# A fused attention and two-expert kernel: first expert in three passes, fewer early weights, more attention buffers

## The chip, the cores and the metric

One core of one Trainium2 chip runs the whole program. The metric is the device time of one execution in microseconds (us). The kernel before has a median of 669.59 us over three runs (669.0 to 670.03).

## What is computed

Shapes: batch 2, 8 heads, 768 positions, head size 64, so 1536 tokens of width 512. All weights come as float64 and are turned into float32 on the chip.

```python
keep = is_global | is_local            # 8 global keys, the last 96 positions
scores = np.where(keep, q @ k.T / 8 + bias, -1e9)
x = softmax(scores) @ v                # (1536, 512)
h = x @ w_in                           # w_in (512, 2048)
x = (h * np.tanh(softplus(h))) @ w_out # first expert, w_out (2048, 512)
g, val = x @ w_gate, x @ w_val         # (512, 1536) each
out = (g * sigmoid(g) * val) @ w_out2  # second expert, w_out2 (1536, 512)
```

## The kernel before, in words

**Order of the work.** The program is first written down as a list of operations (`op`), each with the engines that can do it and a cost in ns. `Plan.order` then places them on the engines in the order of a due time: the sum of the TensorE costs written down before the operation (`nominal`), plus 7000 for other engines, made earlier where a later operation needs it in time. An operation that can run on several engines (a "copy" on ACT or DVE, say) is placed on the one that the plan holds free sooner. Each engine and SP's DMA queue then run their own list in that fixed order and wait for each other by semaphores. Buffers come from pools (`Pool`), handed out in the order in which they were asked for; an operation that finds none is held back, and so are those behind it in that pool.

**Attention.** 12 tiles of 128 positions, 6 per batch, each in two halves of 4 heads (24 half tiles, `s`). For each half: `transp` (L440) turns k and q of the tile by 4 TensorE transposes into one bank and copies the bank to `kq`, which has places 0 and 1 for the keys of the last two tiles and place 2 for the queries (L454, on ACT or DVE); `qk` (L469) makes the scores against the keys of this tile and the one before (L480); `softmax` (L485) adds the bias and takes the row limit on DVE (L499) and the exponential on ACT (recorded at helper line L329); `turn` (L528) transposes the weights by 4 to 8 TensorE transposes (L541) into two banks and copies them to `et`; `spread` (L508) turns the reciprocals of the row sums (L522) into `rs`; `pv` (L551) multiplies with v (L562), scales (L570) and splits the result into a high and a low part of the token block `xt`. A copy by ACT is recorded at L352, one by DVE or POOL at L349. The transposes and pv take their PSUM banks from one pool, `t_p`, with 3 banks. Banks 0 to 3 hold scores, bank 7 is for warm-up matmuls.

**Warm-up.** `warm_up` (L590) writes down 6 matmuls on zeros (L596) that run first, and LATE = 24 more with a due time after everything else: the plan places one wherever it holds TensorE idle.

**Weights.** A unit is 128 x 512 float64 numbers: one column block of w_in, or the matching rows of w_out. `convert` (L392) brings it in by a DMA of 512 KB (L402), takes the absolute value on ACT (L404), does four steps on DVE (L887 to L890) and splits it into a high and a low part (L349 or L352, then L362) in a slot of `w_p`. There are NWA = 13 slots from the start, and NWB = 15 more that take the memory of attention when all of attention is over (`switch`). In the attention loop `units_to` writes down up to 9 units, one per tile from s = 5 on.

**Experts.** Tokens go in 3 chunks of 512. A job is one chunk and one block of 128 hidden columns. `hidden` makes 12 matmuls from `x` (three products of the high and low parts, 4 blocks of the width), then the activation on ACT and DVE (`mish`, L698, or `swiglu`), then 12 matmuls into four output banks `ys` (`out_b`, L759). All of these matmuls are recorded at helper line L373. Jobs of the first expert go in pairs (`jobs_b`, L736), which share the activation's table loads. The 16 column blocks of the first expert go in two passes of 8: for each pass all three chunks, and for each chunk the 8 blocks. The first job of a pass and chunk starts the output banks, the last one empties them: in the first pass by a copy to `st` and a DMA to `part1`, in the second by a DMA from `part1`, an addition on DVE and the split into `xt` on POOL. The 12 blocks of the second expert go in two passes of 6.

What sets how early a job can run: its `h_p` banks (banks 0 to 3, once all scores are done), the output banks (4 to 7, after `switch`), and its units. Unit 2f is the block f of w_in, unit 2f + 1 that of w_out. Requests for `h_p` banks are served in the order of the jobs.

```python
453  copy(lambda: kq.t[:, prs, c:3:2 - c, :], ...)        # keys to place c, queries to place 2
483  pe(emit, [(kq, (c, hf)) for c in (2, 0, 1)[:nb + 1]], ...)
599  op([("P", 216, emit)], ..., prio=-1e5 if i < first else 1e6)
827  units_to(min(9, max(0, (s - 3)//2)))
845  for fs, whole in ((range(0, FA), False), (range(FA, F1), True)):
846      for c in range(NCH):
847          seq += [(1, c, f, f == fs[0], f == fs[-1], whole) for f in fs]
```

Of the kernel before, what the change touches and what calls it, by code (L numbers as in the profile page):

```python
# [219 lines left out]
def kernel(  # L220
# [21 lines left out]
    KD = DM // P  # L242
    CH = 512
    NCH = NTOK // CH
    FA = F1 // 2
    NWA = 13
    NWB = 15
    NST = 2
    WARM = 6
    LATE = 24  # L250
    EDGE = 104
    SPARE = 2500.0
    SCALE = -1.0 / float(D) ** 0.5
# [18 lines left out]
    def fixed(pool, shape, dtype, name):  # L272
        return Buf(t=pool.tile(shape, dtype, name=name))

    def slots(pool, n, shape, dtype, name):
        return [Slot(pool.tile(shape, dtype, name=f"{name}{i}")) for i in range(n)]
# [15 lines left out]
    h_p = Pool([])  # L292
    y_p = Pool([])

    kq = fixed(asb, [P, NP, 3, P], F32, "kq")
    e_p = Pool(slots(asb, 3, [P, 4, 256], F32, "e"))
    et_p = Pool(slots(asb, 5, [P, 2, 2, P], F32, "et"))
    rb_p = Pool(slots(asb, 2, [P, NP, P], F32, "rb"))
    raw_in = {n: Pool(slots(asb, 2, [P, H, D], F32, "in_" + n)) for n in "qkvu"}
    xs_p = Pool(slots(asb, 2, [P, NP, P], F32, "xs"))  # L300
    rs_p = Pool(slots(asb, 1, [P, NP * P], F32, "rs"))
    bias = fixed(asb, [P, H, 3 * P], BF16, "bias")
    bias0 = fixed(asb, [P, H, P], BF16, "bias0")
    kg = fixed(asb, [P, NP, WG], F32, "kg")
# [4 lines left out]
    sm_p = Pool(slots(asb, 3, [P, H], F32, "sm"))  # L309
    asb.tile([P, EDGE], I32, name="edge")  # L310

    asb_pools = [*raw_in.values(), e_p, sm_p, et_p, rb_p, xs_p, rs_p, t_p, warm_p]
    asb_fixed = [bias, bias0, kq, kg, mn, nt, nf, chk]

    def of_attention(o):
# [17 lines left out]
    def dve(emit, r, w, n=512, fast_=False):  # L333
        return op([("V", (150 if fast_ else 68) + (0.52 if fast_ else 1.045) * n, emit)], r, w)

    def dma(emit, r, w, kb=256, prio=None):
        return op([("S", 150 + kb * 4.2, emit)], r, w, lat=2000.0, prio=prio)

    def pe(emit, r, w, mms, n=512, shape="FF", spare=0.0):
        o = op([("P", mms * (max(n, 230) / 2.4 + 13.5), emit)], r, w)  # L340
        o.shape, o.spare = shape, spare
        return o
# [4 lines left out]
    def copy(o, i, r, w, scale=1.0, n=512, psum_in=False, on="AVG"):  # L347
        def dve_pool(eng):
            return lambda: eng.tensor_scalar(out=o(), in0=i(), scalar1=scale, scalar2=0.0, op0=ALU.mult, op1=ALU.add)  # L349

        alts = [("A", (50 if psum_in else 92) + 0.835 * n,
                 lambda: nc.scalar.activation(out=o(), in_=i(), func=AF.Copy, scale=scale)),  # L352
                ("V", (68 + 1.045 * n) if psum_in else (180 + 0.52 * n), dve_pool(nc.vector))]
        if not psum_in:
            alts.append(("G", 160 + 0.88 * n, dve_pool(nc.gpsimd)))
        o_ = op(some(alts, on), r, w)
        o_.port = not psum_in
        return o_
# [56 lines left out]
    def load(i, names="qk"):  # L415
        b, t = tiles[i]
        for nm, src in (("q", q), ("k", k), ("v", v)):
            if nm not in names:
                continue
            x = plan.buf(raw_in[nm])  # L420
            raws[nm, i] = x
            for hs in (slice(0, 4), slice(4, 8)) if i == 0 else (slice(0, H),):
                dma(lambda x=x, src=src, hs=hs: nc.sync.dma_start(
                    out=x.t[:, hs], in_=src[b, hs, t * P:(t + 1) * P, :].rearrange("h s d -> s h d")), [],
                    [(x, hf) for hf in range(hs.start // 4, hs.stop // 4)], kb=32 * (hs.stop - hs.start),
                    prio=-1e6 + hs.start + 9 * (nm == "v") if i == 0 else None)
# [13 lines left out]
    def transp(i, hf):  # L440
        b, t = tiles[i]
        xk, xq = raws["k", i], raws["q", i]
        ps = plan.buf(t_p)
        c = t % 2
        prs = slice(2 * hf, 2 * hf + 2)

        def emit():
            for p in range(4):
                x = xq if p % 2 else xk
                h = 4 * hf + p // 2 * 2  # L450
                nc.tensor.transpose(ps.t[:, p * P:(p + 1) * P], x.t[:, h:h + 2, :].rearrange("s h d -> s (h d)"), ident)  # L451

        pe(emit, [(xk, hf), (xq, hf)], [(ps, 0)], 4, 128)
        copy(lambda: kq.t[:, prs, c:3:2 - c, :], lambda: ps.t.rearrange("p (a b s) -> p a b s", a=2, b=2), [(ps, 0)],  # L454
             [(kq, (c, hf)), (kq, (2, hf))], psum_in=True, on="AV")

    def move_k(i, hf):
        b, t = tiles[i]
# [10 lines left out]
    def qk(s):  # L469
        i, hf = divmod(s, 2)  # L470
        b, t = tiles[i]
        nb = 1 if t == 0 else 2
        banks = scs[s] = [plan.buf(sc_p[0]), plan.buf(sc_p[1])]

        def emit():
            for p in range(2):
                pr = 2 * hf + p
                for j in range(2):
                    ro = slice(64 * j, 64 * j + 64)
                    nc.tensor.matmul(out=banks[j].t[:, p * 256:p * 256 + nb * P], lhsT=kq.t[ro, pr, 2, :],  # L480
                                     rhs=kq.t[ro, pr, 0:nb, :].rearrange("p b s -> p (b s)"), start=True, stop=True)

        pe(emit, [(kq, (c, hf)) for c in (2, 0, 1)[:nb + 1]], [(banks[0], 0), (banks[1], 0)], 8, 230, "RR")

    def softmax(s):  # L485
        i, hf = divmod(s, 2)
# [272 lines left out]
    def out_b(kind, c, f, first, last, whole, g, w, ds):  # L759
        for d in ds:  # L760
            if first:
                ys[d] = plan.buf(y_p)
            y = ys[d]
            blk = slice(d * P, (d + 1) * P)

            def emit(y=y, blk=blk):
                if kind == 1:
                    mm3(y.t, lambda a: w.t[:, a, blk], lambda b: g.t[:, b, :], first, last)
                else:
                    mm3(y.t, lambda a: g.t[:, a, blk], lambda b: w.t[:, b, :], first, last)  # L770

            pe(emit, [(w, 0), (w, 1), (g, 0), (g, 1)], [(y, 0)], 3, CH, spare=SPARE)
            if not last:
                continue
            st = plan.buf(st_p)
            Y, T = [(y, 0)], [(st, 0)]
            if not whole:
                part, pk = (part1, p1) if kind == 1 else (part2, p2)
                copy(lambda st=st: st.t, lambda y=y: y.t, Y, T, scale=1.0 if kind == 1 else 0.5, psum_in=True, on="AV")
                dma(lambda st=st, d=d, part=part: nc.sync.dma_start(out=part[c, d], in_=st.t), T, [(pk, (c, d))])  # L780
            elif kind == 1:
                dma(lambda st=st, d=d: nc.sync.dma_start(out=st.t, in_=part1[c, d]), [(p1, (c, d))], T)
                dve(lambda st=st, y=y: tt(st.t, y.t, st.t, ALU.add), Y, T)
                ks = lambda a: [(xt[c], (a, d, t)) for t in range(CH // P)]
                copy(lambda d=d: xt[c].t[:, 0, d, :], lambda st=st: st.t, T, ks(0), on="G")
                arith(lambda d=d: xt[c].t[:, 1, d, :], lambda st=st: st.t,
                      lambda d=d: xt[c].t[:, 0, d, :].bitcast(F32), ALU.subtract, T + ks(0), ks(1), on="G")
            else:
                dma(lambda st=st, d=d: nc.sync.dma_start(out=st.t, in_=part2[c, d]), [(p2, (c, d))], T)
                dve(lambda st=st, y=y: nc.vector.scalar_tensor_tensor(out=st.t, in0=y.t, scalar=0.5, in1=st.t,  # L790
                                                                      op0=ALU.mult, op1=ALU.add), Y, T)
                r = c * CH + d * P
                dma(lambda st=st, r=r: nc.sync.dma_start(out=out[r:r + P, :], in_=st.t), T, [])


    setup()
    load(1)
    transp(0, 0)
    transp(0, 1)
# [2 lines left out]
    def units_to(n):  # L802
        while n_units[0] < min(n, len(units), freed[0] + room[0]):
            convert(n_units[0])
            n_units[0] += 1

    NS = 2 * NTL
    for s in range(NS + 2):
        i, hf = divmod(s, 2)
        if s < NS:  # L810
            if hf == 0:
                load_previous(i)
                if i + 1 < NTL:
                    load(i + 1, "v")
            qk(s)
            softmax(s)
            move_k(i, hf)
            if i + 1 < NTL:
                transp(i + 1, hf)
            if hf == 1 and i + 2 < NTL:  # L820
                load(i + 2)
        if 0 <= s - 1 < NS:
            turn(s - 1)
            if s % 2 == 0:
                spread(s // 2 - 1)
                pv(s // 2 - 1)
        units_to(min(9, max(0, (s - 3)//2)))
        if s == NS:
            flag()
    def switch():  # L830
# [11 lines left out]
       grow=[(w_p, wb_slots), (st_p, st_slots), (y_p, bank[4:8])])  # L842
    room[0] += NWB
    seq = []
    for fs, whole in ((range(0, FA), False), (range(FA, F1), True)):
        for c in range(NCH):
            seq += [(1, c, f, f == fs[0], f == fs[-1], whole) for f in fs]
    for fs, whole in ((range(0, F2 // 2), False), (range(F2 // 2, F2), True)):
# [281 lines left out]
```

## Time and profile before

| | us |
|---|---|
| median of 3 runs | 669.59 (669.0 to 670.03) |
| the profiled execution, its own time | 668.81 |
| its span, first to last instruction | 667.0 |
| first expert matmul starts | 99.53 |
| last expert matmul ends | 660.57 |

A row of the profile names the engine (PE is TensorE's matmuls, PEld its weight loads, DVE VectorE, ACT ScalarE, POOL GpSimd, SP the DMA queue), the line, and `out<-in` by the program's names. Matmuls are pipelined: the mean duration of one is longer than the distance from start to start, so the time that a run of matmuls takes is read from the chain of waits or from the starts.

### The profile page before, as it was taken

What the parts mean: (1) busy time and instruction counts of PE and PEld (TensorE: products, weight loads), DVE (VectorE), ACT (ScalarE), POOL (GpSimd) and SP (SyncE); (2) the same over time, 40 slices, a digit from 0 to 9 for tenths busy, and PEclk for the clock granted to TensorE, in tenths of its full rate; (3) what the DMA queues carried; (4) which work ended last, traced back from release to release, by engine and by line L of the source; (5) the groups of instructions that cost most, each with busy time, mean ns of one, the idle gap of its engine ahead of it and who ended that gap; (6) DMA issues with size and microseconds to landing.
All of it is one profiled execution on the core that took longest, in us unless ns stands there. A gap on an engine that the chain in (4) does not pass through costs nothing.

```text
span 667.0 us, 9142 instructions
## 1 busy us (share of the span) xinstructions
PE 652.8 (98%) x3343; PEld 535.9 (80%) x3343; DVE 410.5 (62%) x831; ACT 351.1 (53%) x636; POOL 109.7 (16%) x168
## 2 busy tenths in 40 slices
PE   8998999999999999999999999999999999999996
PEld 6876778878888888888888888888888888888884
DVE  5788887888678685797688877222842223323313
ACT  6999997878766776867685333212521211111111
POOL 4343542112111110150251410000000000000000
PEclk9999999999999999999999999999999999999999
DMA  8677641433325234243132224100400300300301
GB/s 197 171 174 179 168 129 63 127 127 130 117 70 179 73 132 153 94 143 124 51 127 93 97 70 142 72 1 1 148 10 16 111 0 17 111 0 17 110 1 68
DMA packets 80068, 63.58 MB, mean 95 GB/s; under 512 B 48272, under 2 KB 68752, under 8 KB 80016
## 3 DMA queue, kind: packets, MB, share of 16 engines
q1 hardware_dynamic: 80016, 62.93, 30.8%
q8 instruction: 28, 0.46, 0.3%
q14 instruction: 24, 0.20, 0.1%
HBM read 53.48 MB, written 9.44 MB: 94 GB/s over the span
## 4 chain that ended last, share of the span: by engine, by line
PE 89%; ACT 5%; DVE 2%; DMA 2%; issue 1%; SPq 0%; ACTq 0%; DVEq 0%
PE bank L373 78%; PE bank L562 3%; PE bank L480 3%; PE bank L541 2%; PE bank L451 2%; DMA raw<-in_moe_w_out_dram 1%; ACT e L329 1%; ACT et L352 1%; PE bank L596 1%; PE bank L522 1%; ACT kq L352 1%; ACT cv L404 1%; DMA in_k<-in_k_dram 1%; ACT u L329 0%; DVE a L362 0%
## 5 line engine op out<-in xcount | busy, mean ns | idle before, releaser
L373 PE MATMUL bank<-x,wa 128*128 128x512 f32 x756 | 180.8, 390 | 1.3 <-DVE a L362 1.3
L373 PEld LDWEIGHTS bank<-x,wa 128*128 128x128 f32 x756 | 141.7, 188 | 31.3 <-DVE a L362 1.7
L373 PE MATMUL bank<-x,wb 128*128 128x512 f32 x684 | 163.5, 390 | 0.0
L373 PEld LDWEIGHTS bank<-x,wb 128*128 128x128 f32 x684 | 128.4, 188 | 26.6
L329 ACT ACTIVATE u<-bank 128x512 f32<-128x512 f32 x84 | 49.9, 594 | 133.4 <-PE bank L373 133.2
L352 ACT ACTIVATE g<-a 128x512 fp32r<-128x512 f32 x64 | 40.3, 632 | 109.9 <-DVE a L729 93.7
L727 DVE SCALAR_TENSOR_TENSOR a<-u,bank 128x512 f32<-128x512 f32 x36 | 24.7, 687 | 92.0 <-ACT u L329 91.9
L362 DVE TENSOR_TENSOR g<-a,g 128x512 fp32r<-128x512 f32 x84 | 61.0, 738 | 22.5 <-ACT g L352 19.3
L373 PE MATMUL bank<-wa,g 128*128 128x512 f32 x288 | 70.2, 389 | 0.0
L373 PE MATMUL bank<-g,wb 128*128 128x512 f32 x288 | 69.0, 389 | 0.0
L373 PE MATMUL bank<-g,wa 128*128 128x512 f32 x288 | 68.9, 390 | 0.0
L373 PEld LDWEIGHTS bank<-g,wa 128*128 128x128 f32 x288 | 54.1, 188 | 11.2
L373 PEld LDWEIGHTS bank<-g,wb 128*128 128x128 f32 x288 | 54.1, 188 | 11.2
L373 PEld LDWEIGHTS bank<-wa,g 128*128 128x128 f32 x288 | 54.1, 188 | 11.2
L729 DVE TENSOR_TENSOR a<-a,bank 128x512 f32<-128x512 f32 x36 | 24.7, 687 | 49.4 <-PE bank L373 49.3
L889 DVE SCALAR_TENSOR_TENSOR cv<-raw,cv 128x512 int32<-128x512 int32 x68 | 48.4, 717 | 0.9
L404 ACT ACTIVATE cv<-raw 128x512 f32<-128x512 f32 x68 | 44.8, 665 | 7.7 <-DMA raw<-in_moe_w_out_dram 4.6
L887 DVE TENSOR_SCALAR cv<-cv 128x512 f32<-128x512 f32 x68 | 35.0, 516 | 22.3 <-ACT cv L404 22.1
L890 DVE SCALAR_TENSOR_TENSOR cv<-raw,cv 128x512 int32<-128x512 int32 x68 | 47.5, 706 | 0.8
L329 ACT ACTIVATE e<-e,mn 128x256 f32<-128x256 f32 (+1 forms) x96 | 46.1, 490 | 1.1 <-DVE mn L499 0.8
L349 POOL TENSOR_SCALAR g<-a 128x512 fp32r<-128x512 f32 x20 | 13.2, 659 | 202.6 <-DVE a L729 125.8
L362 DVE TENSOR_TENSOR a<-bank,u 128x512 f32<-128x512 f32 x48 | 31.1, 686 | 18.9 <-ACT u L329 18.4
(92 smaller groups left out, 748.0 us busy)
## 6 DMA issues: line engine op xcount, KB each, us to landing
raw<-in_moe_w_out_dram SPq DMA_DIRECT2D x28, 512.0 KB, 3.3
raw<-in_moe_w_in_dram SPq DMA_DIRECT2D x16, 512.0 KB, 3.8
raw<-in_moe_w_gate_dram SPq DMA_DIRECT2D x12, 512.0 KB, 3.7
raw<-in_moe_w_val_dram SPq DMA_DIRECT2D x12, 512.0 KB, 3.6
part<-st SPq DMA_DIRECT2D x12, 256.0 KB, 2.1
part<-sb SPq DMA_DIRECT2D x12, 256.0 KB, 2.1
st<-part SPq DMA_DIRECT2D x12, 256.0 KB, 2.8
sb<-part SPq DMA_DIRECT2D x12, 256.0 KB, 3.7
```

The source lines that it names most:

```text
L329: nc.scalar.activation(out=o(), in_=i(), func=func, scale=scale, **args)
L352: lambda: nc.scalar.activation(out=o(), in_=i(), func=AF.Copy, scale=scale)),
L362: return lambda: eng.tensor_tensor(out=o(), in0=x(), in1=y(), op=alu)
L373: nc.tensor.matmul(out=o, lhsT=lhs(a), rhs=rhs(b), start=first and i == 0, stop=last and i == len(PASSES) - 1)
L404: op([("A", 520, lambda: nc.scalar.activation(out=wf(), in_=hi().bitcast(F32), func=AF.Abs))], R, W_)
L480: nc.tensor.matmul(out=banks[j].t[:, p * 256:p * 256 + nb * P], lhsT=kq.t[ro, pr, 2, :], rhs=kq.t[ro, pr, 0:nb, :].rearrange("p b s -> p ( ...
L562: nc.tensor.matmul(out=o.t[64 * j:64 * j + 64, p * P:(p + 1) * P], lhsT=v_of(c).t[:, 2 * p + j, :], rhs=et4[p].t[:, c, j, :], start=c == 0 ...
L727: dve(lambda: nc.vector.scalar_tensor_tensor(out=a.t, in0=u.t[:, 0], scalar=1.0, in1=hg.t, op0=ALU.add, op1=ALU.mult), U + [(hg, 0)], A_)
L729: dve(lambda: nc.vector.tensor_tensor(out=a.t, in0=a.t, in1=hv.t, op=ALU.mult), [(hv, 0)], A_)
L887: lambda: ts(out=f(), in0=f(), scalar1=F64_LOW, scalar2=F64_HIGH, op0=ALU.max, op1=ALU.min),
L889: lambda: stt(out=w(), in0=high(), scalar=-0x40000000, in1=w(), op0=ALU.bitwise_and, op1=ALU.bitwise_or),
L890: lambda: stt(out=w(), in0=low(), scalar=29, in1=w(), op0=ALU.logical_shift_right, op1=ALU.bitwise_or),
```

## The change

The first expert's 16 column blocks go in passes of 4, 4 and 8 instead of 8 and 8. The middle pass brings the partial sum in, adds and writes it back (12 more DMA loads, additions and DMA stores of 256 KB). Up to 5 units instead of 9 are written down in the attention loop, from s = 7 on instead of s = 5, and the slots that exist from the start are 10 instead of 13 (18 instead of 15 come after attention). The 12 KB per partition that this frees pay for a fourth buffer of `e`, a sixth of `et`, a second of `rs` and a second place for turned queries. There are 6 late warm-up matmuls instead of 24, with a due time near 0 through the operation that follows them, and when they are done bank 7 joins `t_p` as its fourth bank.

```diff
--- before.py
+++ after.py
@@ -242,12 +242,12 @@
     KD = DM // P
     CH = 512
     NCH = NTOK // CH
-    FA = F1 // 2
-    NWA = 13
-    NWB = 15
+    PASSES1 = (0, 4, 8)
+    NWA = 10
+    NWB = 18
     NST = 2
     WARM = 6
-    LATE = 24
+    LATE = 6
     EDGE = 104
     SPARE = 2500.0
     SCALE = -1.0 / float(D) ** 0.5
@@ -292,13 +292,13 @@
     h_p = Pool([])
     y_p = Pool([])
 
-    kq = fixed(asb, [P, NP, 3, P], F32, "kq")
-    e_p = Pool(slots(asb, 3, [P, 4, 256], F32, "e"))
-    et_p = Pool(slots(asb, 5, [P, 2, 2, P], F32, "et"))
+    kq = fixed(asb, [P, NP, 4, P], F32, "kq")
+    e_p = Pool(slots(asb, 4, [P, 4, 256], F32, "e"))
+    et_p = Pool(slots(asb, 6, [P, 2, 2, P], F32, "et"))
     rb_p = Pool(slots(asb, 2, [P, NP, P], F32, "rb"))
     raw_in = {n: Pool(slots(asb, 2, [P, H, D], F32, "in_" + n)) for n in "qkvu"}
     xs_p = Pool(slots(asb, 2, [P, NP, P], F32, "xs"))
-    rs_p = Pool(slots(asb, 1, [P, NP * P], F32, "rs"))
+    rs_p = Pool(slots(asb, 2, [P, NP * P], F32, "rs"))
     bias = fixed(asb, [P, H, 3 * P], BF16, "bias")
     bias0 = fixed(asb, [P, H, P], BF16, "bias0")
     kg = fixed(asb, [P, NP, WG], F32, "kg")
@@ -309,7 +309,7 @@
     sm_p = Pool(slots(asb, 3, [P, H], F32, "sm"))
     asb.tile([P, EDGE], I32, name="edge")
 
-    asb_pools = [*raw_in.values(), e_p, sm_p, et_p, rb_p, xs_p, rs_p, t_p, warm_p]
+    asb_pools = [*raw_in.values(), e_p, sm_p, et_p, rb_p, xs_p, rs_p, t_p]
     asb_fixed = [bias, bias0, kq, kg, mn, nt, nf, chk]
 
     def of_attention(o):
@@ -451,8 +451,8 @@
                 nc.tensor.transpose(ps.t[:, p * P:(p + 1) * P], x.t[:, h:h + 2, :].rearrange("s h d -> s (h d)"), ident)
 
         pe(emit, [(xk, hf), (xq, hf)], [(ps, 0)], 4, 128)
-        copy(lambda: kq.t[:, prs, c:3:2 - c, :], lambda: ps.t.rearrange("p (a b s) -> p a b s", a=2, b=2), [(ps, 0)],
-             [(kq, (c, hf)), (kq, (2, hf))], psum_in=True, on="AV")
+        copy(lambda: kq.t[:, prs, c:4:2, :], lambda: ps.t.rearrange("p (a b s) -> p a b s", a=2, b=2), [(ps, 0)],
+             [(kq, (c, hf)), (kq, (2 + c, hf))], psum_in=True, on="AV")
 
     def move_k(i, hf):
         b, t = tiles[i]
@@ -477,10 +477,10 @@
                 pr = 2 * hf + p
                 for j in range(2):
                     ro = slice(64 * j, 64 * j + 64)
-                    nc.tensor.matmul(out=banks[j].t[:, p * 256:p * 256 + nb * P], lhsT=kq.t[ro, pr, 2, :],
+                    nc.tensor.matmul(out=banks[j].t[:, p * 256:p * 256 + nb * P], lhsT=kq.t[ro, pr, 2 + t % 2, :],
                                      rhs=kq.t[ro, pr, 0:nb, :].rearrange("p b s -> p (b s)"), start=True, stop=True)
 
-        pe(emit, [(kq, (c, hf)) for c in (2, 0, 1)[:nb + 1]], [(banks[0], 0), (banks[1], 0)], 8, 230, "RR")
+        pe(emit, [(kq, (c, hf)) for c in (2 + t % 2, 0, 1)[:nb + 1]], [(banks[0], 0), (banks[1], 0)], 8, 230, "RR")
 
     def softmax(s):
         i, hf = divmod(s, 2)
@@ -774,7 +774,11 @@
                 continue
             st = plan.buf(st_p)
             Y, T = [(y, 0)], [(st, 0)]
-            if not whole:
+            if kind == 1 and whole == 1:
+                dma(lambda st=st, d=d: nc.sync.dma_start(out=st.t, in_=part1[c, d]), [(p1, (c, d))], T)
+                dve(lambda st=st, y=y: tt(st.t, y.t, st.t, ALU.add), Y, T)
+                dma(lambda st=st, d=d: nc.sync.dma_start(out=part1[c, d], in_=st.t), T, [(p1, (c, d))])
+            elif not whole:
                 part, pk = (part1, p1) if kind == 1 else (part2, p2)
                 copy(lambda st=st: st.t, lambda y=y: y.t, Y, T, scale=1.0 if kind == 1 else 0.5, psum_in=True, on="AV")
                 dma(lambda st=st, d=d, part=part: nc.sync.dma_start(out=part[c, d], in_=st.t), T, [(pk, (c, d))])
@@ -794,6 +798,8 @@
 
 
     setup()
+    op([("X", 0, lambda: None)], after=[o for o in plan.ops if any(b.pool is warm_p for b in o.bufs)], lat=0.0, prio=0.0,
+       grow=[(t_p, bank[7:8])])
     load(1)
     transp(0, 0)
     transp(0, 1)
@@ -824,7 +830,7 @@
             if s % 2 == 0:
                 spread(s // 2 - 1)
                 pv(s // 2 - 1)
-        units_to(min(9, max(0, (s - 3)//2)))
+        units_to(min(5, max(0, (s - 5) // 2)))
         if s == NS:
             flag()
     def switch():
@@ -842,7 +848,9 @@
        grow=[(w_p, wb_slots), (st_p, st_slots), (y_p, bank[4:8])])
     room[0] += NWB
     seq = []
-    for fs, whole in ((range(0, FA), False), (range(FA, F1), True)):
+    for n, f0 in enumerate(PASSES1):
+        fs = range(f0, (PASSES1 + (F1,))[n + 1])
+        whole = (n > 0) + (fs[-1] == F1 - 1)
         for c in range(NCH):
             seq += [(1, c, f, f == fs[0], f == fs[-1], whole) for f in fs]
     for fs, whole in ((range(0, F2 // 2), False), (range(F2 // 2, F2), True)):
```

## Rows read from the trace of the kernel before

**Rows 1.** Busy time, the line of all engines on the profile page.

```profile
PE 652.8 (98%) x3343; PEld 535.9 (80%) x3343; DVE 410.5 (62%) x831; ACT 351.1 (53%) x636; POOL 109.7 (16%) x168
```

**Rows 2.** The chain that ended last, in order of time: start, us, what.

```profile
6.85 1.28 PE bank L596 x3
...
10.14 0.69 PE bank L596 x3
...
41.31 0.47 PE bank L596 x2
...
50.12 2.95 ACT e L329 x12
...
99.60 5.70 PE bank L373 x24
...
148.88 511.69 PE bank L373 x2256
```

**Rows 3.** Busy time by stretch: us, PE, PEld, DVE, ACT, POOL, granted clock, DMA.

```profile
45.00:57.50 12.50, 11.27 (x113) 9.17 (x112) 10.68 (x46) 12.44 (x38) 5.43 (x9) 1.00 0.85 209
...
9.70:99.50 89.80, 85.76 (x823) 67.77 (x822) 74.30 (x275) 84.43 (x273) 38.30 (x73) 1.00 0.69 172
...
149.00:660.60 511.60, 511.55 (x2256) 423.41 (x2256) 290.77 (x469) 224.52 (x304) 59.83 (x69) 1.00 0.24 79
```

**Rows 4.** What PE waited for from 9 to 150 us: total, times, longest.

```profile
PE bank L373 <- DVE a L362: 1.3, 1, 1.3
PE bank L541 <- ACT kq L352: 1.1, 2, 0.8
PE bank L541 <- ACT et L352: 1.0, 2, 0.5
...
PE bank L451 <- ACT et L352: 0.7, 1, 0.7
PE bank L522 <- ACT kq L352: 0.5, 1, 0.5
```

**Rows 5.** Groups of instructions on ACT and DVE from 9.7 to 99.5 us.

```profile
L352 ACT ACTIVATE et<-bank 128x512 f32<-128x512 f32 x37 | 20.7, 595 | 1.0 <-PE bank L541 0.7
L404 ACT ACTIVATE cv<-raw 128x512 f32<-128x512 f32 x9 | 6.1, 675 | 0.0
...
L889 DVE SCALAR_TENSOR_TENSOR cv<-raw,cv 128x512 int32<-128x512 int32 x8 | 5.7, 718 | 0.0
L349 DVE TENSOR_SCALAR kq<-bank 128x512 f32<-128x512 f32 x4 | 2.8, 692 | 2.0 <-PE bank L451 1.3 <-ACT e L329 0.5
```

**Rows 6.** PE in order of time, the first microseconds.

```profile
1.47 3.36 PE L596 MATMUL bank<-g 128*128 128x512 f32 x7 [1.47 <-DVE g L593]
5.76 0.45 PE L451 MATMUL bank<-ident,in_k 128*128 128x128 f32 x1 [0.94 <-DMA in_k<-in_k_dram]
```

**Rows 7.** DVE in order of time: three units are finished after attention's last score.

```profile
103.21 0.68 DVE L362 TENSOR_TENSOR wa<-cv,wa 128x512 fp32r<-128x512 f32 x1
...
109.43 0.69 DVE L362 TENSOR_TENSOR wa<-cv,wa 128x512 fp32r<-128x512 f32 x1 [0.74 <-POOL wa L349]
...
120.03 0.68 DVE L362 TENSOR_TENSOR wa<-cv,wa 128x512 fp32r<-128x512 f32 x1
```

**Rows 8.** PE in order of time, the first jobs of the first expert.

```profile
99.53 5.76 PE L373 MATMUL bank<-x,wa 128*128 128x512 f32 x24
...
106.96 3.00 PE L373 MATMUL bank<-x,wa 128*128 128x512 f32 x12
...
111.89 5.76 PE L373 MATMUL bank<-x,wa 128*128 128x512 f32 x24
...
125.65 5.60 PE L373 MATMUL bank<-g,wa 128*128 128x512 f32 x24
```

**Rows 9.** DMA issues of partial sums: line, count, KB, us to landing.

```profile
part<-st SPq DMA_DIRECT2D x12, 256.0 KB, 2.1
...
sb<-part SPq DMA_DIRECT2D x12, 256.0 KB, 3.7
```

## The prediction

> **What bounds the kernel now.** I read the busy line first. PE is busy for 98% of the span [rows 1], so time can go only where PE waits or does work that nobody needs. The chain in order of time shows where that is: from 148.88 us on, 2256 matmuls of the experts run with nothing between them for 511.69 us [rows 2], 226.8 ns each, and PE is busy for 511.55 of 511.60 us there, at a granted clock of 1.00 [rows 3]. The experts have 2448 matmuls; 2448 x 0.2268 = 555.2 us is a floor that the change doesn't touch. The first of them starts at 99.53 us [rows 8], and from there to 148.88 us PE's one wait is the 1.3 us at the end, for a DVE result of an activation [rows 4]. So the prizes are two: attention before 99.53 us, and that 1.3 us.
>
> In the stretch from 9.70 to 99.50 us (89.80 us) PE is busy for 85.76, ACT for 84.43 and DVE for 74.30 us [rows 3]. PE's 85.76 hold 20 late warm-up matmuls: the chain has them in ten pieces, from the 0.69 us at 10.14 to the 0.47 us at 41.31, 5.48 us together [rows 2]. So the real work of attention on PE is 80.3 us, and 4.0 us are idle. Of this idle time 3.3 us end with an ACT copy (1.1 + 1.0 + 0.7 + 0.5) [rows 4]: a transpose waits for the copy that empties its bank. ACT is the other bound: from 45.0 to 57.5 us it is busy for 12.44 of 12.50 us, and there the chain runs through its exponentials [rows 2, 3].
>
> **The change, part by part.**
>
> *Late dummies, 24 to 6.* The 20 that ran after 9.7 us go. They lay on the chain, so 5.48 us of PE time come free; PE's idle time grows by whatever they covered, which I settle below through ACT. Their due time now lies near zero, so the five left after the first seven run as soon as PE is free, between the first transposes and the first scores, where three ran before in 1.28 us [rows 2]. Two more at that stage's distance of 0.48 us (3.36 us for seven [rows 6]) cost 1.0 us before the first scores; I take that. The ends: nothing, if the first exponentials wait for something else anyway, and 12 x 0.48 = 5.8 us from 1.47, so 7.3 instead of 5.76, if they all run ahead of the first transposes, 1.5 us [rows 6].
>
> *Nine early units to five.* The stretch held nine absolute values on ACT and eight to nine of every DVE step [rows 5]. Four fewer take 4 x 0.675 = 2.7 us from ACT, 2.3 without the overlap of neighbours, and from DVE some 4 x 3 us (one step is 0.72 [rows 5]; four steps and a subtraction). ACT is left with 84.4 - 2.3 = 82.1 us. A DVE with 12 us less to do will be given more of the copies that either engine may take; of ACT's `et` and `kq` copies (37 at 0.595 [rows 5] in the larger group) I let three go over, about 0.48 us each from start to start: 80.7 us. The ends are no copy, and as many as bring ACT under PE's 80.3.
>
> *Fourth bank, fourth `e`, sixth `et`, second `rs`.* They add no instruction. They let PE run one copy further ahead, which is worth at most the 3.3 us of bank waits. They don't shorten the ACT work, so I count them only in how well the bound engine is used.
>
> *Second place for queries.* Nearly nothing: keys and queries leave the bank in one copy. The key place it overwrites is that of the tile before last, which the scores of the present tile still read wherever they take two blocks of keys. Only after tile 0 of each batch, 2 of 11 transitions, is the copy free earlier.
>
> *The sum for attention.* PE has 80.3 us of work, ACT 80.7; the larger counts, plus its idle time. Over the whole stretch ACT idled 89.80 - 84.43 = 5.4 us, in its tight part 0.06 [rows 3]. With the extra buffers I take 3.0, between them. That makes 83.7 where 89.8 stood, 6.1 us less; less the 1.0 at the start, the first expert begins 5.1 us earlier. If PE alone bounds and nothing idles, 9.5 us earlier; if ACT loses only its 2.3 us and the dummies' time becomes waiting, 1.3.
>
> *Passes of 4, 4 and 8.* With T the first expert matmul, the eight-block pass needed units 8 to 15 within its first four pairs of jobs, and the chain's wait of 1.3 us is the end of that supply. Now pairs three to six reuse units 0 to 7, for four times some 10.9 us (48 matmuls), and the supply has time. I count the 1.3 us as gained. No matmul is added. New are 12 loads of partial sums, 12 additions and 12 stores. A load lands in 2.8 to 3.7 us and a store in 2.1 [rows 9], one set of four per chunk, and a chunk's two pairs of jobs are 21.8 us of matmuls; the addition costs DVE about 0.7 us as the others on a full bank do, 8 us in all, and DVE is idle for 221 of the 511.6 us after 149 [rows 3]. A store waits on SP's queue for its addition, and weight loads stand behind it, but the units of the next pass are then tens of us from their use. I count nothing; if that cover went, one set would cost a load's 3.7 us for each of three chunks, 11 us.
>
> *Units 5 to 7 later.* Third column block: unit 4, ready. The fourth needs unit 6 for its first matmuls, the second half of the 24 at 111.89, so T + 15 at the latest in today's order, T + 12.4 if the halves swap [rows 8]. Units 5 and 7 are wanted at 125.65, T + 26 [rows 8]. Before, the three units finished after T landed at T + 4.4, + 10.6 and + 21.2 (103.21, 109.43 and 120.03 plus 0.68 [rows 7]). If units 5, 6 and 7 take these places, all are in time, by 1.8 us at the tightest. I take zero. The low end is zero too, since an earlier unit finds PE at work; the high end is unit 6 in the third place, 8.8 us late.
>
> *Sum.* 5.1 + 1.3 = 6.4 us off the profiled execution's 668.81 us: 662.4. That execution lies 0.8 us under the median of 669.59, inside the runs' own spread.
>
> **A rule against it.** PE without dummies is seen between 45.0 and 57.5 us: it idles there for 1.2 of 12.5 us, its longest single wait in all of attention is 0.8 us, and the granted clock stays at 1.00, the 2.4 GHz level [rows 3, 4]. The Trainium skill (TensorE: Matmul & The Clock Gate, Part 1: The HAM clock gate) says that a TensorE left idle falls back to half its clock, which is what dummies prevent; by it, thinning them is a risk, worked out below as a rival. The rows so far show no fall at such gaps.
>
> **The rivals.**
> - *ACT stays the bound.* No copy moves over and the dummies' time turns into waits for ACT. For: 12.44 of 12.50 us. Against: DVE stands idle for 15.5 of 89.8 us. Attention gains 2.3 - 1.0 = 1.3, the experts 1.3: 666.2.
> - *Unit 6 is late.* `h_p` banks go out in the order of the jobs, so a fourth column block without its weights also holds back pair three, whose weights are there. Unit 6 in the third place stalls PE by 8.8 us: 668.8 - 6.4 + 8.8 = 671.2, slower. It decides against the change once unit 6 lands more than 6.4 us (7.2 against the median) after T + 12.4. For: four units fewer stand ready. Against: the plan makes units early by their use, and DVE has time in attention for one or two beyond five.
> - *The clock falls* to 1.2 GHz somewhere in attention. PE's own work fills 80.3 of 89.8 us, so each 10 us of today's order at the lower level hold 8.9 us that take twice as long: 668.8 - 6.4 + 8.9 = 671.3 with one such piece.
> - *Nothing in sum*: the parts do what they say, and stalls of the middle pass's partial sums, two of 3.7 us, eat it: 668.8 - 6.4 + 7.4 = 669.8.
>
> **How the numbers follow.** The forecast has 0.60, ACT as the bound 0.24, unit 6 late 0.08, the clock 0.03, nothing in sum 0.05. About 0.2% (1.3 us) is what a measurement of this kernel can tell from no change. The first two are faster (0.84), the late unit and the clock are slower (0.11), the last lies within 0.2% of the median (0.05). For the range: the low end is attention bound by PE alone, 668.8 - 9.5 - 1.3 = 658.0; the upper end takes in ACT as the bound with the experts' gain lost as well (667.5) and half a us for the runs' spread, 668.0. Some 0.16 lie above it and a few hundredths below.
>
> **What would show it.** The first expert matmul at about 94.4 us instead of 99.53. No L596 after the first 11 us. From 10 us to there, ACT busy for over 95% and more DVE copies of `et` and `kq` than the four of now. No PE wait between the first expert matmul and the last, whose chain then has over 2400 matmuls in one piece. No more waits of L541 for `kq` copies. Wrong would be: T within 2 us of the old one; a PE wait of L373 for a unit's DVE subtraction within 20 us after T; a wait of L373 behind an addition of partial sums; a granted clock under 0.95 in any stretch of attention.

## The result, and the profile after

| | before | after |
|---|---|---|
| median, us | 669.5 (669.0 to 670.03, 4 runs) | 662.0 (661.35 to 662.26, 4 runs) |
| span of the profiled execution | 667.0 | 660.4 |
| first expert matmul by the chain, T | 99.60 | 94.32 |
| last expert matmul ends | 660.57 | 652.89 |

The ratio is 0.989, with a 95% interval of 0.9876 to 0.9903. The forecast was 662.4 us, with T at 94.4 us. Every T from here on is read from the chain, where the kernel before has 99.60 us [rows 2]; by the start of the instruction it is 99.53 [rows 8], and 94.08 for the kernel after.

The chain that ended last, of the kernel after, in order of time (start, us, what):

```profile
5.81 0.64 PE bank L451 x4
6.45 0.02 issue
6.48 0.60 ACT kq L352
7.08 3.21 ACT bias L352 x14
...
93.30 1.02 PE bank L541 x8
94.32 5.49 PE bank L373 x24
99.82 0.87 PE bank L541 x8
100.69 0.44 PE bank L522 x4
101.13 2.77 PE bank L373 x12
103.90 0.11 PE bank L672
104.01 1.90 PE bank L562 x32
105.91 546.98 PE bank L373 x2412
652.89 0.02 issue
652.91 0.69 DVE sb L794
```

T lies 5.28 us earlier. From 105.91 us on 2412 expert matmuls run in one piece, 226.8 ns each as before; the wait of 1.3 us [rows 4] is gone, and so from T to the last matmul there are 558.57 us instead of 560.97. Of the other 1.1 us of that difference 0.2 are the first 24 matmuls, in 5.49 us instead of 5.70 [rows 2], and some 0.6 what is left over from attention, with four transposes fewer (L541, 8 where 12 stood). From the last matmul to the end of the span there are 7.5 us instead of 6.4. This tail varies between 6.2 and 7.5 us over the profiles of this study, whose instructions there are the same; nothing in them says why. 5.28 + 2.40 - 1.08 = 6.6 us is what the spans differ by.

Busy time of the kernel after by stretch (columns as in [rows 3]), the tight part of before and attention from 9.7 us to T:

```profile
45.00:57.50 12.50, 12.31 (x137) 10.04 (x136) 10.60 (x39) 12.22 (x44) 6.59 (x11) 1.00 0.73 178
...
9.70:94.30 84.60, 80.81 (x805) 64.88 (x806) 69.88 (x261) 79.77 (x265) 38.03 (x68) 1.00 0.68 170
```

What PE waited for from 9 us on, of the kernel after (total, times, longest):

```profile
PE bank L541 <- ACT et L352: 1.7, 3, 0.7
PE bank L451 <- DMA in_k<-in_k_dram: 0.9, 1, 0.9
PE bank L522 <- POOL rb L516: 0.6, 2, 0.4
PE bank L451 <- ACT et L352: 0.6, 1, 0.6
PE bank L480 <- issue: 0.4, 1, 0.4
PE bank L480 <- ACT kq L352: 0.4, 1, 0.4
```

Against [rows 3], PE's work of attention is what it was without dummies (80.81, where 85.76 held 5.48 of them), and ACT has 79.77 instead of 84.43 us. In the stretch where ACT was the bound and PE busy for 11.27 of 12.50 us, PE now has 12.31, though the order differs and so the instructions in it aren't the same ones. The waits of L541 and L522 for `kq` copies [rows 4] are gone, and no wait of L373 is left.

### The profile page after: what moved, and what is told of

It is laid out like the page before. It is cut to its first block, busy times and chain, and to the rows that moved or that the text cites. A ratio compares the mean times of both kernels' runs of the same rounds, so it can differ in the third digit from the quotient of the medians.

```text
span 660.4 us, 9154 instructions
## 1 busy us (share of the span) xinstructions
PE 645.8 (98%) x3325; PEld 531.5 (80%) x3325; DVE 417.5 (63%) x844; ACT 351.7 (53%) x640; POOL 110.0 (17%) x163
## 4 chain that ended last, share of the span: by engine, by line
PE 95%; ACT 2%; DMA 1%; issue 0%; POOL 0%; SPq 0%; DVE 0%; ACTq 0%; POOLq 0%
PE bank L373 84%; PE bank L480 3%; PE bank L562 3%; PE bank L541 3%; PE bank L451 1%; ACT e L329 1%; PE bank L522 1%; ACT et L352 1%; DMA in_k<-in_k_dram 1%; ACT bias L352 0%; ACT kq L352 0%; POOL rb L516 0%; ACT cv L404 0%; DVE sb L794 0%; POOL x L349 0%
## 5 line engine op out<-in xcount | busy, mean ns | idle before, releaser
L373 PE MATMUL bank<-x,wb 128*128 128x512 f32 x864 | 206.1, 389 | 0.0
L373 PEld LDWEIGHTS bank<-x,wb 128*128 128x128 f32 x864 | 162.2, 188 | 33.6
L373 PE MATMUL bank<-x,wa 128*128 128x512 f32 x576 | 137.3, 390 | 0.0
L373 PEld LDWEIGHTS bank<-x,wa 128*128 128x128 f32 x576 | 107.9, 188 | 22.5 <-issue 0.2
L373 PE MATMUL bank<-g,wb 128*128 128x512 f32 x324 | 78.0, 389 | 0.0
L373 PEld LDWEIGHTS bank<-g,wb 128*128 128x128 f32 x324 | 60.8, 188 | 12.6
L373 PE MATMUL bank<-g,wa 128*128 128x512 f32 x252 | 60.2, 389 | 0.0
L373 PEld LDWEIGHTS bank<-g,wa 128*128 128x128 f32 x252 | 47.3, 188 | 9.8
L373 PE MATMUL bank<-wb,g 128*128 128x512 f32 x216 | 54.0, 389 | 0.0
L373 PE MATMUL bank<-wa,g 128*128 128x512 f32 x216 | 52.2, 389 | 0.0
L373 PEld LDWEIGHTS bank<-wa,g 128*128 128x128 f32 x216 | 40.6, 188 | 8.4
L373 PEld LDWEIGHTS bank<-wb,g 128*128 128x128 f32 x216 | 40.5, 188 | 8.4
```

Source lines behind the costliest of these rows:

```text
L373: nc.tensor.matmul(out=o, lhsT=lhs(a), rhs=rhs(b), start=first and i == 0, stop=last and i == len(PASSES) - 1)
```

## The experiments

Each was timed beside the kernel before, whose medians there were 668.66 to 668.88 us; where two of these runs are compared, their ratios are the safer measure. T and PE's waits between T and 160 us are from the one profile of each run. The column "clock" says how that profile starts, which is explained under the first run.

| run | median, us | ratio to before (95%) | T | expert waits | clock |
|---|---|---|---|---|---|
| kernel before | 669.5 | 1 | 99.60 | 1.3 | late |
| kernel after | 662.0 | 0.989 (0.9876 to 0.9903) | 94.32 | 0 | early |
| passes only | 667.14 | 0.9978 (0.997 to 0.9987) | 98.64 | 0 | early |
| dummies only | 671.23 | 1.0039 (1.0026 to 1.0052) | 95.88 | 4.7 | early |
| passes and dummies | 665.05 | 0.9944 (0.993 to 0.9957) | 96.71 | 0 | late |
| after, two passes of 8 | 675.83 | 1.0109 (1.0094 to 1.0124) | 94.73 | 8.8 | late |
| after, five slots | 669.04 | 1.0005 (0.9995 to 1.0015) | 94.72 | 5.2 | late |
| after, nine early units | 663.87 | 0.9922 (0.9908 to 0.9935) | 95.98 | 0 | late |
| after, three banks | 661.52 | 0.9896 (0.9881 to 0.9912) | 94.30 | 0 | early |
| after, three banks, 24 dummies | 662.99 | 0.991 (0.9894 to 0.9925) | 95.81 | 0 | early |
| after, old buffers | 661.92 | 0.9896 (0.9881 to 0.9911) | 94.77 | 0 | late |
| after, one query place | 659.89 | 0.9869 (0.9854 to 0.9884) | 92.66 | 0 | late |
| after, due time 7100 | 662.54 | 0.9908 (0.9893 to 0.9923) | 94.64 | 0 | early |
| after, pv cost | 660.23 | 0.9876 (0.9861 to 0.9891) | 93.24 | 0 | late |

The first question was which part carries the gain, and whether the supply of weights is a bound of its own.

**Passes only.**

```diff
 (kernel before)
-    FA = F1 // 2
+    PASSES1 = (0, 4, 8)
...
+            if kind == 1 and whole == 1:
...
+                dma(lambda st=st, d=d: nc.sync.dma_start(out=part1[c, d], in_=st.t), T, [(p1, (c, d))])
```

> The kernel before with the first expert in passes of 4, 4 and 8 and nothing else changed. Theory: the attention stage is the same, first expert matmul at 99.5 us, and the 1.3 us wait of the experts is gone: 668.2 us, 1.3 below before. Rival (the extra partial sums cost time): a wait of L373 behind an addition or a load of partial sums, 669.5 or more.

It gained 1.7 us, and the chain holds all later matmuls in one piece:

```profile
98.64 5.70 PE bank L373 x24
...
111.03 546.98 PE bank L373 x2412
```

So the 1.3 us go and the 12 more partial sums cost nothing that shows. T is 1.0 us earlier although PE runs the same instructions in the same order up to there. What differs is the start: PE in order of time in this run, and [rows 6] for before.

```profile
5.75 0.30 PE L451 MATMUL bank<-ident,in_k 128*128 128x128 f32 x1 [1.07 <-DMA in_k<-in_k_dram]
5.89 0.27 PE L451 MATMUL bank<-ident,in_q 128*128 128x128 f32 x1
```

Here the first transposes stand 0.14 us apart and take 0.27 to 0.30 us; in the profile of before the first took 0.45 us and the second started 0.24 us after it. A stretch's granted clock can't show this: it reads 1.00 in both there, since the trace holds no record of the clock before its first rise. That record begins at 4.40 us in this run, at 5.41 in the kernel after and at 9.81 in the kernel before. So these transposes ran at the 2.4 GHz level here and not yet before.

The fourteen profiles fall into two kinds: the clock rises at 4.4 to 5.4 us in six of them ("early") and at 9.0 to 10.4 in the others ("late"). One and the same order of PE's instructions is found in both kinds, so the kernel doesn't decide it. What the late rise cost wasn't the same in each order: 0.96 us of T in that of before, 0.83 in that with fewer dummies (96.71 against 95.88), and 0.4 in that of the kernel after, which three late runs share up to T (two passes of 8, five slots, old buffers: 94.72 to 94.77 against 94.32).

The profile of after is early, that of before late. Like with like, the change moved T by 4.3 us (98.64 to 94.32, both early) to 4.9 us (99.60 to 94.73, both late).

**Dummies only.**

```diff
 (kernel before)
-    LATE = 24
+    LATE = 6
```

> The kernel before with 6 late warm-up matmuls instead of 24, their due time and the banks as before. Theory (PE bound from 10 to 45 us, so the dummies' 5.5 us lay on the path): the first expert matmul 3 to 4.5 us earlier, 665 to 666.5 us. Rival (ACT bound, the dummies filled waits): within 1 us of before, 668.5 to 669.5 us, with PE waiting for ACT where the dummies were.

Neither. T came 3.7 us earlier, but 2.8 against the run above, which had the same start: a little less than the theory's 3 to 4.5. And yet the run was 2.4 us slower than before. PE in order of time, and busy time by stretch with the granted clock in the column before the last two:

```profile
139.47 5.60 PE L373 MATMUL bank<-g,wa 128*128 128x512 f32 x24
149.27 7.11 PE L373 MATMUL bank<-x,wa 128*128 128x512 f32 x24 [4.20 <-DVE a L362]
156.21 2.88 PE L373 MATMUL bank<-g,wb 128*128 128x512 f32 x12
```

```profile
139.00:144.00 5.00, 5.00 (x24) 4.13 (x22) 2.09 (x4) 4.94 (x6) 0.62 (x1) 1.00 0.51 166
144.00:149.00 5.00, 1.07 (x5) 0.56 (x3) 1.33 (x3) 4.96 (x6) 0.00 (x0) 0.98 0.00 0
149.00:154.00 5.00, 4.73 (x15) 3.82 (x16) 5.00 (x11) 2.18 (x5) 0.00 (x0) 0.68 0.01 3
```

The run of 2256 matmuls starts at 149.27 us, where it started at 148.88 before [rows 2]: all that attention gave, the first pass of eight blocks lost again. Its units 8 to 15 were finished only 0.8 to 3.5 us earlier than before, the last of them at 138.67 us instead of 139.47. The chain goes back from the wait through the activations of two pairs, one behind the other on ACT, to the transfer of a unit whose absolute value stands ahead of them in ACT's order:

```profile
132.99 3.75 DMA raw<-in_moe_w_in_dram
...
137.99 1.28 ACT L708
...
143.22 1.28 ACT L708
```

The wait grew to 4.2 us, and after it the granted clock was at the lower level for a while: 24 matmuls took 7.1 us instead of 5.7, which makes the loss 1.4 us larger.

**Passes and dummies together** tests that reading.

```diff
 (the run with passes only)
-    LATE = 24
+    LATE = 6
```

> The kernel before with both the passes of 4, 4 and 8 and 6 late warm-up matmuls, each of which has run alone. Theory (fewer dummies bring the first expert matmul 2.8 us forward, which the supply of weights ate where the first pass had 8 blocks, and the cut takes that bound away): 1.7 + 2.8 us less than before, 664 to 665 us, first expert matmul at about 95.9 us, no wait of the experts. Rival (the two just add): 667.1 + 2.4 = 669.5 us.

Measured 665.05 us, 3.6 us under before, where the two alone give -1.7 and +2.4; the theory's 664 to 665 us is met but for 0.05. No wait of L373 is left. Its T of 96.71 us was taken with the late rise of the clock, that of 95.88 us of the run with dummies only, whose order up to T is the same, with the early one. So the cut of the passes is not worth 1.3 us: it is what lets the earlier T count.

**The new kernel with two passes of 8.**

```diff
 (kernel after)
-    PASSES1 = (0, 4, 8)
+    PASSES1 = (0, 8)
```

> The new kernel with two passes of 8, as before. Attention as in the new kernel, first expert matmul at 94.3 us. Theory (the first pass of 8 needs units 8 to 15 within four pairs of jobs, and five early units leave the supply two to three units behind the kernel before): PE waits for units between 94 and 150 us, 6 to 10 us in all, 668 to 672 us. Rival (the cut is worth only the 1.3 us of before): 663.3 us.

T was 94.73 us, and the run was 13.8 us slower than the kernel after, more than the theory had. PE in order of time:

```profile
129.70 4.62 PE L373 MATMUL bank<-x,wb 128*128 128x512 f32 x12 [2.82 <-POOL wb L349]
135.11 5.74 PE L373 MATMUL bank<-x,wa 128*128 128x512 f32 x24 [0.79 <-DVE a L362]
...
153.33 4.83 PE L373 MATMUL bank<-x,wa 128*128 128x512 f32 x13 [4.33 <-DVE a L362]
```

The waits are 8.8 us, with one of 0.9 us ahead of these lines. After the wait of 2.8 us and after that of 4.3, matmuls ran at the lower level (12 took 4.6 us and 13 took 4.8, where 12 take 2.9), and not after the one of 0.8; that is a good part of the rest. Two things make the supply short here: the earlier T, and that 5 units are finished by T where the kernel before and the run with dummies only have 8. Two passes of 8 with nine early units weren't run, so the shares of the two aren't shown.

**Five slots: units 5 to 7 made late.**

```diff
 (kernel after)
-    NWA = 10
-    NWB = 18
+    NWA = 5
+    NWB = 23
```

> The new kernel with 5 weight slots from the start and 23 after attention, so that units 5, 6 and 7 can't be finished before attention's memory is free, about 15 us after the first expert matmul T; they land at about T + 17 to T + 20. Theory (banks for the first half of a job go out in the order of the jobs, so the fourth column block without its weights holds back the next pair too): PE waits 5 to 7 us from T + 11.5 on, 667 to 669 us. Rival (the next pair, whose weights are there, fills the gap): 662 to 663 us.

Measured 669.04 us, 7.0 more than after: a late unit 6 eats the gain, as the prediction's rival had it. PE in order of time, and the three units on DVE:

```profile
107.68 5.78 PE L373 MATMUL bank<-x,wa 128*128 128x512 f32 x24 [1.39 <-DVE a L362]
...
113.97 2.88 PE L373 MATMUL bank<-x,wb 128*128 128x512 f32 x12
...
125.39 4.61 PE L373 MATMUL bank<-x,wa 128*128 128x512 f32 x12 [3.78 <-DVE a L362]
```

```profile
110.59 1.88 DVE L362 TENSOR_TENSOR wb<-cv,wb 128x512 fp32r<-128x512 f32 x3
```

The three units end together at 112.5 us, T + 17.8. The waits are 5.2 us, split in two, and again matmuls at the lower level follow the longer one (12 in 4.6 us). The way to them is only in part the theory's. The next pair did go ahead of the late block: its 24 matmuls start at 107.68 us, 3.6 us before unit 6 is finished (111.88) and after a wait of 1.4 us for a bank (what ends it is DVE's `a`, which reads one), and the late block's 12 follow at 113.97. So the order of the banks held PE for 1.4 us; the wait of 3.8 us comes after that, with the activation of the late pair behind that of the next pair on ACT (table loads, L708, at 119.35 and 114.11 us).

**Nine early units.**

```diff
 (kernel after)
-        units_to(min(5, max(0, (s - 5) // 2)))
+        units_to(min(9, max(0, (s - 3)//2)))
```

> The new kernel with nine early units from s = 5 on, as before. Theory (only two conversions less lie in attention, because the plan makes units ahead wherever DVE is free, so the number written down matters little): first expert matmul 0.5 to 1.5 us later than 94.3 us, no wait of the experts, 662.5 to 663.5 us. Rival (the four units are what eased ACT and DVE): 2.5 us or more later, 664.5 us or more.

T is 95.98 us, 1.7 later, and the time 1.9 us more (0.0032 in the ratios, 2.1 us). Its profile has the late rise of the clock; against 94.73 us, the late T of the order of after, it is 1.3 us, within the theory. The time lies between the theory and the rival.

**The banks, the dummies in the new kernel, the buffers, the query place.** Four runs of single parts:

```diff
 (three banks: kernel after)
-    op([("X", 0, lambda: None)], after=[...warm_p...], ..., grow=[(t_p, bank[7:8])])
...
 (three banks, 24 dummies: the same, and)
-    LATE = 6
+    LATE = 24
 (old buffers: kernel after, e 4 to 3, et 6 to 5, rs 2 to 1)
-    e_p = Pool(slots(asb, 4, [P, 4, 256], F32, "e"))
+    e_p = Pool(slots(asb, 3, [P, 4, 256], F32, "e"))
...
 (one query place: kernel after)
-    copy(lambda: kq.t[:, prs, c:4:2, :], ...
+    copy(lambda: kq.t[:, prs, c:3:2 - c, :], ...
...
```

> The new kernel without the step that gives bank 7 to the transposes: three banks, 6 late warm-up matmuls with their old due time after everything. Theory (the fourth bank is worth part of the 3.3 us of bank waits, since ACT bounds as well): first expert matmul 0.5 to 2 us later than 94.3 us, 662.5 to 664 us, more waits of PE for ACT copies. Rival (the bank is what frees attention): 3 us or more later, 665 us or more.

> The run with three banks, and 24 late warm-up matmuls as before. Against that run it tells what the 18 dummies cost in the new kernel, where no weight supply hides it. Theory (they lay on PE's path): 3 to 4.5 us more than the run with three banks. Rival (they filled waits): within 1 us of it.

> The new kernel with three buffers of e, five of et and one of rs, as before. Theory (they only smooth the order): 0 to 1.5 us more than the new kernel, 662 to 663.5 us. Rival (they are what let PE run ahead): 2.5 us or more, 664.5 us or more.

> The new kernel with one place for the turned queries, as before. Theory (keys and queries leave the bank in one copy, whose key place the scores of the present tile still read; 2 of 11 transitions are freed): within 0.7 us of the new kernel, 661.5 to 662.7 us. Rival (the place separates the tiles): 2 us or more later.

Without the fourth bank, and with the old due time of the six dummies, T is 94.30 us and the time 661.52: the two together are worth nothing that shows. The 18 dummies cost 1.5 us, in T (95.81 against 94.30) as in time (662.99 against 661.52), half of what the theory had; the intervals of the two ratios overlap, the two T agree with the difference. Without the buffers the time is the same; PE's instructions up to T come in the very order of the kernel after, and T is 94.77 where that order has 94.73 with the same late start. With one query place the kernel is faster, 659.89 us, and T is 92.66, late: 2.1 us under that 94.73, a miss to the side that neither theory had.

**A control.**

```diff
 (kernel after)
-    SLACK = 7000.0
+    SLACK = 7100.0
```

> A control: the new kernel with the due time of all other engines than TensorE 7100 instead of 7000, which changes nothing but the order that the plan finds. It tells how much of a difference of single parts is the order's accident. Theory: 0 to 1 us to either side of 662 us. If it moves by 2 us or more, the single parts of attention can't be told apart by such runs.

It moved by 0.5 us in the medians, and by 0.0018 (1.2 us) in the ratio to the kernel before of its own call. T moved by 0.3 us, both early. So a single part that moves the time by about 1 us can't be told from the order that the plan happens to find, and one control shows only one other order. The bank and the buffers are below that. The query place isn't clearly above it: 0.0021 in the ratio to the kernel after, with intervals that overlap, and 2.1 us of T. The plan finds another order with it, nothing that the instructions wait for explains why fewer places should be faster, and whether the place or the order did it isn't shown.

What can be told of T's 4.9 us, late start with late start: fewer dummies 2.9 (99.60 to 96.71), the other parts together 2.0 (to 94.73), of which nine early units, in one run with an order of its own, give back 1.3.

**The cost of pv in the plan.**

```diff
 (kernel after)
-           4 * nb, 230, "CC")
+           9 * nb, 230, "CC")
```

> The new kernel with the plan's cost of one pv of 32 matmuls raised from 0.88 to 1.97 us, what the trace shows is 1.90. Theory (the plan holds TensorE free where it is not, so its order lets ACT and DVE wait on TensorE): first expert matmul 0.5 to 2 us earlier, 660 to 661.5 us. Rival (TensorE's work in attention, 80.8 of 84.6 us, is the bound whatever the order): within 0.5 us of 662 us.

660.23 us with T at 93.24: 1.8 us faster in the medians, 0.0014 in the ratios, whose intervals overlap. T is late, and 1.5 us under the late 94.73, which speaks for the theory; the control limits this as it does the query place.

## Why the prediction was right, and where it was not

*Attention, 5.1 us.* T was forecast at 94.4 and is 94.32. That the two agree to 0.1 us is luck: like with like the change moved T by 4.3 to 4.9 us, and the late start of before against the early one of after did the rest. The bound of the sum was ACT, by 0.4 us; in the kernel after PE has a little more (80.8 against 79.8 us). PE's work came out as said (80.8 for 80.3 us), and the idle time that it bears is 3.8 us where 3.0 was taken. The idle time before was read a little short: all 4.0 us of it, not 3.3, end with an ACT copy, for pv waited too:

```profile
PE bank L562 <- ACT et L352: 0.7, 1, 0.7
```

ACT came to 79.77 us where 80.7 was forecast, by another way. "Nine early units to five", step "four fewer", failed: only two went, as the groups of the kernel after from 9.7 to 94.3 us show:

```profile
L404 ACT ACTIVATE cv<-raw 128x512 f32<-128x512 f32 x7 | 4.6, 679 | 0.3 <-DMA raw<-in_moe_w_out_dram 0.3
```

```profile
L349 DVE TENSOR_SCALAR kq<-bank 128x512 f32<-128x512 f32 x6 | 4.0, 685 | 1.4 <-PE bank L451 1.4
...
L349 DVE TENSOR_SCALAR et<-bank 128x512 f32<-128x512 f32 x2 | 1.4, 687 | 0.9 <-PE bank L541 0.9
```

Seven absolute values, not five: the plan makes units ahead wherever DVE is free, written down early or not. In place of the two others more copies went from ACT to DVE than the three I gave: two more of `kq`, two of `et` and two of `rs`. Two absolute values and six copies at some 0.5 us are the larger part of the 4.7 us that ACT lost.

*Late dummies, 5.48 us.* As work on PE they went, as said. As time they were worth 2.8 us of T in the old kernel (early starts; 2.9 with late ones) and 1.5 in the new one. The 1.0 us for two more cold dummies is about the right size where the clock rises late: in the run with two passes, whose order to T is that of the kernel after, the first scores began at 8.97 us instead of 8.13. In the kernel after itself the dummies aren't on the chain, which was the low end given: it runs there through ACT's `bias` copies (7.08 us) and not through a dummy.

*Passes, 1.3 us.* The wait went and the partial sums cost nothing, so the term held in the sum. But it was taken as what the cut is worth, and it is that only while T stays where it was. With the new T and five units ready at it the uncut passes wait for 8.8 us and the cut is worth 13.8 (675.83 - 662.0). The terms of the sum were not independent: the 5.1 us hung on the cut.

*Units 5 to 7.* Forecast at T + 4.4, + 10.6 and + 21.2. DVE of the kernel after, in order of time:

```profile
97.02 1.29 DVE L362 TENSOR_TENSOR wa<-cv,wa 128x512 fp32r<-128x512 f32 x2
106.56 0.68 DVE L362 TENSOR_TENSOR wa<-cv,wa 128x512 fp32r<-128x512 f32 x1
```

They landed at T + 3.4, + 4.0 and + 12.9, earlier than taken, because two of them were begun in attention. PE's matmuls that need unit 6 are in the 36 that start at 105.84, T + 11.5. Unit 6, at T + 4.0, was there 7.5 us before its matmuls, so the rival of the late unit didn't come about. The run with five slots shows what it would have cost: 7.0 us where 8.8 was taken, by waits of 1.4 and 3.8 us and matmuls at the lower clock, not by one stall.

*Second query place, nearly nothing.* Not a gain, which was right; but the kernel without it was faster, which I had not reckoned with, and the cause stays open.

*The rivals.* ACT as the bound fell: PE is busy for 80.8 of 84.6 us and ACT for 79.8. That is 94.3% for ACT, so this one of the signs, "over 95%", was missed. The clock did not fall in attention (1.00). It does fall, elsewhere: see below.

## What to carry to other kernels

Before time is bought in one stage, look at what feeds the next one: an earlier start is worth nothing where the next stage waits for a supply that doesn't move with it, and a change that looks like a loss alone (here the dummies) can be a gain with the one that removes that bound. So two parts should be tried together and apart, and a part's worth be given with the state of the others. Where a greedy plan sets the order, run a control that changes nothing but the order, and read no single part below what it moves. A T of a single profile is compared with one of the same start: here the early and the late rise of the clock alone were 0.4 to 1.0 us apart.

## What was not expected of the hardware

A long wait of PE costs more than its length. After waits of 2.8, 3.8, 4.2 and 4.3 us the next matmuls ran at the 1.2 GHz level until the clock was granted again, which cost 1.4 us for the 24 after 149.27 us in the run with dummies only. After waits of 0.8 us (two passes of 8) and 1.3 us (before) they did not. The Trainium skill (TensorE: Matmul & The Clock Gate, Part 1: The HAM clock gate) has that fall to half the clock after idleness. These runs agree, and here it is the long waits between T and 154 us that set it off, not the loss of the dummies: the clock stays at 1.00 to the last matmul in the kernel after, which has as few. The same section says that the moment of the first rise varies from run to run. The two kinds of start here, with the rise at 4.4 to 5.4 or at 9.0 to 10.4 us and 0.4 to 1.0 us apart in T at the same order, agree with that.
